# Where the later experts' token lists are read in a planned scan and mixture-of-experts kernel

## The chip, the core and the metric

The kernel runs on one core of a Trainium2 chip. The metric is the device time of one execution, in microseconds (us). Three runs of the kernel before stand beside one execution that the hardware profiler recorded.

## The reference

Three stages follow each other, all in float32.

```
x = gated linear scan(q, k, v, a_re, a_im)     # 4 batches, 8 heads, 768 steps, head size 48
x = (silu(g) * val) @ w_out,  g, val = rmsnorm(x) @ (w_gate, w_val)   # 3072 tokens, 384 -> 1536 -> 384
logits = x @ w_gate2;  e = argmax(logits);  p = softmax(logits)[e]    # 8 experts
out[token] = p * (relu(x @ w1[e]) @ w2[e])                            # 384 -> 1024 -> 384
```

Only the last stage is touched by the change. Each token goes to one of eight experts, so the kernel has to find out at run time which tokens an expert has, bring their rows together, run the two matrix products of that expert, and write the rows back to their places.

## The kernel before

The tokens are worked off in twelve units of 256 tokens. While a unit passes through the dense layer, its rows and logits go to `x2all` in DRAM, and a scatter on GpSimd's queue (L966) writes the number of each token into a list of its expert, in DRAM (`slots`, two tensors, one for each half of the unit). After the unit before the last, the experts are sorted by their counts so far (`sort`, L1033 to L1047); the place in that order is the number by which this text calls them: expert 0 is the largest one, 7 the smallest. Each has a fixed room for its tokens (`CAPS`); what goes beyond it is counted by `beyond` (L1049 to L1068) and worked off by a loop at the very end, which does not run when nothing went beyond.

An expert needs four things. Its **list**: `read_list` (L1124) issues two small loads from `slots` on SyncE's queue (SP, L1129), into one row of the two tiles `idx`, and VectorE joins the two by a minimum (L1132). Its **rows**: `gather` (L1136) issues one indirect load for each 110 to 128 tokens on GpSimd's queue (L1137, tile `ex`). Its **weights**: `load_weights` (L1091) loads seven pieces on SP's queue, three of `w1` (L1106, 512 KB each) and four of `w2` (L1108, 384 KB each), into three raw buffers (`rawb`) that are used in turn; ScalarE makes a rounded high part of each piece (L1113, `h1`, `h2`) and VectorE the rest (L1117, `l1`, `l2`), and only then is the raw buffer free for the load after the next two. And the **products**: TensorE transposes the rows (L1299, `ex`), ScalarE and VectorE split them into `exh` and `exl` (L1303, L1305), stage 1 makes eight column blocks (L1317, tile `m` in PSUM, three buffers), each split by ScalarE and VectorE into `ehh` and `ehl` (L1324, L1326), and stage 2 (L1335, tile `a` in PSUM, two buffers) makes the output, which ScalarE scales (L1341, `eo`) and GpSimd's queue scatters (L1343). Weights of experts with an odd number end in tiles that end in b, those of even ones in tiles that end in a.

Expert 0 is done in two halves: 246 tokens that were listed early (tiles `eh`, `el`), and 246 that are known late, whose rows are gathered into `rawa` and completed by rows of the last unit with matrix products by a selection matrix (`join_late`, L1182 and L1186). The list of expert 1 is completed in the same way (`join_next`), from the list of the units before the last. Experts 2 to 7 read their lists only after the last unit's scatters have landed.

No engine chooses its work at run time. Every instruction is recorded as a step with what it reads and writes, and `Plan.issue` (L185) then writes the instructions out engine by engine: again and again it takes, among the steps whose inputs are planned, one that can start first, ties going to the earlier due time. A step's cost and its `lag` (the time from the issue of a transfer to its landing) are the planner's estimates, and `after=` names further steps that have to be planned before it. All this sets only the order on each engine and queue; at run time each instruction waits for the data that it really touches, and all that stands behind it on its engine waits too. On the DMA queues a further wait is shown in some instructions: for an earlier transfer that uses the same completion semaphore.

Of the kernel before, what the change touches and what calls it, by code (L numbers as in the profile page):

```python
# [41 lines left out]
def act(n):  # L42
    return 0.1 + n / 1200


def dve(n):
    return 0.07 + n / 960


def pool2(n):  # L50
    return 0.15 + n / 460
# [82 lines left out]
class Plan:  # L134
# [5 lines left out]
    def add(self, engs, fn, r=(), w=(), due=0.0, table=None, lag=0.0, after=(), size=0, span=(0.0, math.inf), pull=0.0, lock=False):  # L140

        s = Step()
        s.size, s.span, s.pull, s.lock = size, span, pull, lock
        s.engs = [engs] if isinstance(engs, tuple) else engs
        s.fn, s.due, s.table, s.lag = fn, due, table, lag
        s.next, s.end, s.seq = [], None, len(self.steps)
        deps = {id(a): a for a in after}
        bufs = {}  # L150
        for writes, items in ((False, r), (True, w)):
            for x in items:
                b, part = x if isinstance(x, tuple) else (x, None)
                bufs[id(b)] = b
                for p, (wr, rd) in b.last.items():
                    if p == part or p is None or part is None:
                        for d in ([wr] if wr else []) + (rd if writes else []):
                            deps[id(d)] = d
        for writes, items in ((False, r), (True, w)):
            for x in items:  # L160
                b, part = x if isinstance(x, tuple) else (x, None)
                if writes:
                    if part is None:
                        b.last.clear()
                    b.last[part] = (s, [])
                else:
                    b.last.setdefault(part, (None, []))[1].append(s)
        deps.pop(id(s), None)
        s.bufs = list(bufs.values())
        for b in s.bufs:  # L170
            b.users += 1
        s.deps = list(deps.values())
        s.wait = len(s.deps)
        for d in s.deps:
            d.next.append(s)
        self.steps.append(s)
        return s
# [73 lines left out]
def kernel(ctx, tc, qT, kT, reT, imT, v, wg, wv, wo, rg, w2g, w1, w2, out):  # L251
    nc = tc.nc
    V, A, G, TE, SP = nc.vector, nc.scalar, nc.gpsimd, nc.tensor, nc.sync
    P = 128
# [19 lines left out]
    NJS = tuple(-(-c // P) for c in CAPS)  # L274
# [66 lines left out]
    add = plan.add  # L341

    def dma(fn, nbytes, r=(), w=(), due=0.0, after=(), issue=0.48, lag=TUNE["DL"]):
        return add((SP, issue), fn, r=r, w=w, due=due, lag=lag, size=nbytes, after=after)

    CNT, CARRY, X2ALL, SLOTS, IDENTR, GAIN, W2G, HOT, FIRST, PERM, MORE, SECOND = (Buf(t=1) for _ in range(12))
# [12 lines left out]
    def due_moe(u, f):  # L359
        return T0 + PER * u + FT * f  # L360
# [6 lines left out]
    def due_elem(u):  # L367
        return TUNE[f"EU{min(u, 5)}"] + (TUNE["E0"], T0 + TUNE["E1"], T0 + TUNE["E2"])[u] if u < 3 else T0 + PER * (u - 2) + TUNE["E3"]
# [291 lines left out]
    def attention(u, QK, vt):  # L660
        b, p = units[u]
        xh, xl = Buf(k_xh), Buf(k_xl)
        for c in range(NC):
            chunk(u, c, QK, vt, xh, xl, p == 0 and c == 0, p == NP - 1 and c == NC - 1)
        return xh, xl
# [342 lines left out]
    def due_e(x, i):  # L1008
        return due_moe(NU, 0) + sum(EP[:x]) + i - (TUNE["EL"] if x else 0.0)
# [66 lines left out]
        add((V, 0.1), lambda e: e.scalar_tensor_tensor(out=nk, in0=pc.t, scalar=SCALE, in1=rev,  # L1076
                                                       op0=ALU.mult, op1=ALU.add), r=[pc], w=[MORE], due=due)

    which, told = {}, {}

    def number(x, due):

        def load(e):
            i = x or E
            which[x] = nc.values_load(permi[0:1, i:i + 1], engines=[mybir.EngineType.SP], min_val=0, max_val=E - 1)

        return add((SP, 0.8), load, r=[PERM if x else FIRST], due=due)
# [3 lines left out]
    def load_weights(x, after):  # L1091
        W = [Buf(k) for k in k_w[x % 2]]
        if x not in told:
            told[x] = number(x, due_e(x, -32))
        after = after + [told[x]]
        for m, (src, n) in enumerate(((w1, KD), (w2, KF2 // 2))):
            for k in range(n):
                raw = Buf(k_rb if x else k_ra)
                due = due_e(x, 0) - EP[x - 1 if x else 0] + 4 * m + 0.4 * k - (40 if x == 1 else 0)

                def piece(t, m=m, k=k):
                    return t[:, k, :] if m == 0 else t[:, 2 * k:2 * k + 2, :].rearrange("p k d -> p (k d)")

                def load(e, raw=raw, m=m, k=k):
                    if m == 0:
                        e.dma_start(raw.t, w1r[bass.ds(which[x] * DM + k * P, P), :])  # L1106
                    else:
                        e.dma_start(raw.t[:, :2 * DM].rearrange("p (k d) -> p k d", k=2),  # L1108
                                    w2r[bass.ds(which[x] * F2 + 2 * k * P, 2 * P), :].rearrange("(k p) d -> p k d", p=P))

                cols = F2 if m == 0 else 2 * DM
                dma(load, P * cols * 4, w=[raw], due=due, after=after)
                add((A, act(cols)), lambda e, raw=raw, m=m, piece=piece, cols=cols: e.activation(  # L1113
                    piece(W[2 * m].t), raw.t[:, :cols], AF.Copy),
                    r=[raw], w=[(W[2 * m], k)], due=due, after=after)
                add([(V, dve(cols)), (G, pool2(cols))],
                    lambda e, raw=raw, m=m, piece=piece, cols=cols: e.tensor_tensor(  # L1117
                        out=piece(W[2 * m + 1].t), in0=raw.t[:, :cols], in1=piece(W[2 * m].t), op=ALU.subtract),
                    r=[raw, (W[2 * m], k)], w=[(W[2 * m + 1], k)], due=due, after=after, lock=True)
        return W  # L1120

    lists = [Buf(k) for k in k_idx]

    def read_list(x, row, lo, n, after):  # L1124

        due = due_e(x if x > 1 else 0, -30)
        at = [lambda b=b: b.t[:TPS[x], row, :n] for b in lists]
        for b, t, sl in zip(lists, at, slots):
            dma(lambda e, t=t, sl=sl: e.dma_start(t(), sl[bass.ds(which[x] * NT + lo, n * TPS[x]), :].rearrange(  # L1129
                "(p j) o -> p (j o)", j=n)), 2e3, r=[SLOTS], w=[(b, row)], due=due, after=after + [told[x]])  # L1130
        a, o = at
        add((V, 0.1), lambda e: e.tensor_tensor(out=a(), in0=a(), in1=o(), op=ALU.min),  # L1132
            r=[(lists[1], row)], w=[(lists[0], row)], due=due)
        return row

    def gather(X, j, idx, src, r, due, after, **kw):  # L1136
        add((G, 1.05), lambda e: e.indirect_dma_start(  # L1137
            out=X.t[:, j, :], out_offset=None, in_=src,
            in_offset=bass.IndirectOffsetOnAxis(ap=lists[0].t[:X.shape[0], idx, j:j + 1], axis=0), **kw),
            r=[(lists[0], idx)] + r, w=[(X, j)], due=due, lag=4.4, after=after)  # L1140

    def join_late(row, X):

# [116 lines left out]
    def expert(x, W, idx, n, rooms, due, after, X=None):  # L1260
# [14 lines left out]
        for j in () if there else range(n):  # L1275
            gather(X, j, idx, src, rows, due(-30), after)
# [71 lines left out]
    with tc.manual_schedule():  # L1348
# [31 lines left out]
        for sl in slots:  # L1380
# [11 lines left out]
            r=[GAIN], w=[GAIN], due=due_elem(0) + 1)  # L1392
        dma(lambda e: e.dma_start(w2gt[:, :, :E], w2g.rearrange("(k p) e -> p k e", p=P)), 1e3, w=[W2G],
            due=due_elem(0) + 1)
# [14 lines left out]
        for w, k in order[:int(TUNE["FF"])]:  # L1409
            add((TE, mmr(WB, int(TUNE["FN"]))), lambda e, w=w, k=k: keep_warm(e, w, k), r=[(w, 0), IDENTR], w=[fill],  # L1410
                due=1e6, span=(0.0, TUNE["W1"]))
        x = {0: attention(0, *q[0])}
# [4 lines left out]
        for u in range(NU):  # L1417
# [4 lines left out]
            if u + 1 == NU:  # L1422
                to_right = add((G, 0.0), open_right, after=[s for s in plan.steps if any(
                    b.slots and b.slots.where is right for b in s.bufs)], due=due_moe(u, 0))
                Wn = load_weights(0, [to_right])
            acc = dense(u, *x[u])
            if u + 1 == NU:
# [10 lines left out]
                idx1 = read_list(1, 1, 0, NJS[1], [to_right])  # L1438
# [11 lines left out]
        expert(0, Wn, late, NJ - NE, rooms1, lambda i: due_e(0, i), [to_left], Xl)  # L1450
        for x_ in range(1, E):
            W = load_weights(x_, [to_left])
            idx = idx1 if x_ == 1 else read_list(x_, x_, 0, NJS[x_], [to_right])
            expert(x_, W, idx, NJS[x_], rooms, lambda i, x_=x_: due_e(x_, i), [to_left])
        add((V, 2.0), beyond, r=[PERM, HOT], w=[MORE], due=due_e(2, 0))
        plan.issue()
        for cm in reversed(closers):
            cm.__exit__(None, None, None)
# [3 lines left out]
        with tc.For_i(0, nr, 1):  # L1462
            with tc.tile_pool(name="fb", bufs=1) as fb, tc.tile_pool(name="fp", bufs=2, space=PSUM) as fp:
# [30 lines left out]
                x = fb.tile([R, XW], F32, name="fx")  # L1494
# [30 lines left out]
                o = fb.tile([R, DM], F32, name="fo")  # L1525
# [49 lines left out]
```

## Time and profile before

| what | value |
|---|---|
| median of three runs | 958.65 us (954.86 to 959.91) |
| profiled execution | 958.0 us, of which the span from first to last instruction is 956.3 us |
| mean granted TensorE clock | 0.986 of 2.4 GHz |
| busy: PE, DVE, ACT, POOL | 95%, 66%, 55%, 17% of the span |
| DMA | 98.12 MB, mean 103 GB/s |

PE is TensorE's matmuls, DVE VectorE, ACT ScalarE, POOL GpSimd, SPq SyncE's DMA queue. Busy shares are means over the whole span. The experts' stage lies at its end: the last matmuls of the dense layer run until about 694 us, expert 0 is worked on from there, and the rest follow to the end. What an engine waits for there is read from the views of that stretch, in the section of rows below.

### The profile page before, as it was taken

The page shows a single profiled execution, that of the slowest core. Times are in us where ns is not written, and L with a number is a line of the kernel's source. Part 1 is how long each engine was busy: PE and PEld are TensorE (multiplying, and loading weights), DVE is VectorE, ACT ScalarE, POOL GpSimd, SP SyncE. Part 2 cuts the span into 40 slices and gives each one's busy share as a digit, 9 for nine tenths or more (in the row PEclk, how much of TensorE's full clock was granted, in tenths as well). Part 3 has the DMA queues.
Part 4 walks back from the last instruction along what each step waited for, and adds up shares of the span by engine and source line. Part 5 has one row for each costly group of instructions (what it writes and reads, how often), then busy time and mean ns, then how long its engine had stood idle before and what let it go on. Part 6 is the DMA issues. An engine that isn't in the chain of part 4 may idle for free.

```text
span 956.3 us, 17768 instructions
## 1 busy us (share of the span) xinstructions
PE 906.0 (95%) x6747; PEld 867.7 (91%) x6747; DVE 630.2 (66%) x1534; ACT 528.8 (55%) x1017; POOL 160.5 (17%) x211
## 2 busy tenths in 40 slices
PE   0979999999999999999999999999988999999996
PEld 0769999999999999999999999999877999999996
DVE  5889986878786969586868777446655543534520
ACT  8885775757575666565656575334424443544421
POOL 1223201010011010100101000101173142132121
PEclk9988999999999999999999999999999999999998
DMA  9932416151525060505050413003347554445200
GB/s 340 319 142 70 114 35 133 35 134 35 133 35 133 18 151 17 151 17 151 18 141 19 100 60 62 24 1 85 83 103 203 167 167 119 139 140 177 89 21 23
DMA packets 68363, 98.12 MB, mean 103 GB/s; under 512 B 16038, under 2 KB 49257, under 8 KB 68276
## 3 DMA queue, kind: packets, MB, share of 16 engines
q1 hardware_dynamic: 57316, 86.61, 32.7%
q0 software_dynamic: 10688, 9.95, 4.0%
q8 instruction: 54, 0.88, 0.4%
q10 hardware_dynamic: 272, 0.40, 0.1%
q14 instruction: 33, 0.27, 0.1%
HBM read 68.19 MB, written 10.15 MB: 82 GB/s over the span
## 4 chain that ended last, share of the span: by engine, by line
PE 62%; DVE 11%; issue 10%; ACT 7%; DMA 6%; SPq 2%; POOL 2%; POOLq 0%; DVEq 0%; ACTq 0%
PE m L868 26%; PE a L891 13%; PE a L1335 6%; PE t L698 4%; PE m L1317 3%; PE t L738 3%; DMA rawb<-in_w_dram 3%; DVE re L594 1%; PE t L742 1%; POOL out_dram L1343 1%; DVE ee L559 1%; PE t L716 1%; PE t L823 1%; DMA out_dram<-eo,idx 1%; DVE hl L885 1%
## 5 line engine op out<-in xcount | busy, mean ns | idle before, releaser
L868 PE MATMUL m<-xh,w 128*128 128x256 f32 x1728 | 278.6, 286 | 0.2 <-DVE s L880 0.2
L868 PEld LDWEIGHTS m<-xh,w 128*128 128x128 f32 x1728 | 236.3, 190 | 5.2 <-issue 3.6
L891 PE MATMUL a<-wo,hh 128*128 128x392 f32 (+1 forms) x576 | 152.6, 346 | 0.0
L868 PE MATMUL m<-xl,w 128*128 128x256 f32 x864 | 149.5, 282 | 0.0
L868 PEld LDWEIGHTS m<-xl,w 128*128 128x128 f32 x864 | 123.2, 190 | 0.0
L875 ACT ACTIVATE s<-m 128x256 f32<-128x256 f32 x144 | 54.3, 381 | 88.3 <-PE m L868 54.1
L891 PEld LDWEIGHTS a<-wo,hh 128*128 128x128 f32 x576 | 100.7, 189 | 0.6 <-issue 0.5
L891 PE MATMUL a<-wo,hl 128*128 128x392 f32 (+1 forms) x288 | 98.3, 341 | 2.3 <-DVE hl L885 2.3
L883 ACT ACTIVATE hh<-s 128x256 fp32r<-128x256 f32 x144 | 59.3, 416 | 64.1 <-PE a L891 43.7
L885 DVE TENSOR_TENSOR hl<-s,hh 128x256 fp32r<-128x256 f32 x144 | 63.8, 449 | 25.5 <-ACT hh L883 24.7
L877 DVE SCALAR_TENSOR_TENSOR s<-s,m 128x256 f32<-128x256 f32 x144 | 59.4, 415 | 24.4 <-ACT s L875 24.0
L1343 POOL DMA_INDIRECT out_dram<-eo,idx x28 | 37.1, 1327 | 162.6 <-ACT eo L1341 105.2
L1326 DVE SCALAR_TENSOR_TENSOR ehl<-m,ehh 128x384 fp32r<-128x384 f32 (+6 forms) x64 | 35.0, 555 | 42.1 <-ACT ehh L1324 42.1
L880 DVE SCALAR_TENSOR_TENSOR s<-s,m 128x256 f32<-128x256 f32 x144 | 59.4, 416 | 1.9
L1324 ACT ACTIVATE ehh<-m 128x384 fp32r<-128x384 f32 (+6 forms) x64 | 31.0, 491 | 48.9 <-PE m L1317 47.1
L1341 ACT ACTIVATE eo<-a,eg 114x384 f32<-114x384 f32 (+5 forms) x28 | 16.3, 581 | 73.4 <-PE a L1335 69.8
L891 PEld LDWEIGHTS a<-wo,hl 128*128 128x128 f32 x288 | 54.1, 188 | 2.9 <-DVE hl L885 2.9
L966 POOL DMA_INDIRECT slots<-tid,sl x24 | 25.1, 1046 | 150.7 <-DVE cnt L961 146.7
L738 PE MATMUL t<-AK,vt 128*64 128x224 f32 (+3 forms) x384 | 49.7, 345 | 0.0
L698 PE MATMUL t<-QK 96*128 96x128 f32 x384 | 48.1, 277 | 0.5 <-DMA QK<-ee 0.5
L698 PEld LDWEIGHTS t<-QK 96*128 96x128 f32 x384 | 45.5, 192 | 1.7 <-issue 0.9
L1335 PE MATMUL a<-h2b,ehh 128*118 128x384 f32 (+3 forms) x112 | 37.9, 339 | 0.0
(295 smaller groups left out, 1864.0 us busy)
## 6 DMA issues: line engine op xcount, KB each, us to landing
rawb<-in_w_dram SPq DMA_DIRECT2D x21, 512.0 KB, 7.5
rawb<-in_w_dram SPq DMA_DIRECT2D x28, 384.0 KB, 4.2
QK<-qk SPq DMA_DIRECT2D x24, 290.2 KB
QK<-ee SPq DMA_DIRECT2D x24, 290.2 KB, 6.4
re<-in_a_re_dram SPq DMA_DIRECT2D x12, 384.0 KB
im<-in_a_im_dram SPq DMA_DIRECT2D x12, 384.0 KB
qk<-in_q_dram SPq DMA_DIRECT2D x12, 384.0 KB, 5.1
qk<-in_k_dram SPq DMA_DIRECT2D x12, 384.0 KB, 5.8
```

What stands on the lines that cost most here:

```text
L698: TE.matmul(sc.t[:, i, :], lhsT=K(4 * g + i), rhs=Q(4 * g + i), start=True, stop=True)
L738: TE.matmul(yt.t[64 * n:64 * n + d, i, :n_], lhsT=vs[:, o:o + d], rhs=ak.t[:, 2 * i + n, :n_], start=True, stop=first)
L868: TE.matmul(ps.t[:, i, :], lhsT=W1[i, g].t[:, k, part, fs], rhs=x.t[:, k, :], start=(n == 0), stop=(n == 3 * KD - 1))
L875: add((A, act(U)), lambda e: e.activation(s.t, ps.t[:, 0, :], AF.Tanh, scale=0.5), r=[ps], w=[s], due=dh, table=AF.Tanh)
L877: add((V, dve(U)), lambda e: e.scalar_tensor_tensor(out=s.t, in0=s.t, scalar=1.0, in1=ps.t[:, 0, :], op0=ALU.add, op1=ALU.mult), r=[s, ps] ...
L880: add((V, dve(U)), lambda e: e.scalar_tensor_tensor(out=s.t, in0=s.t, scalar=0.5, in1=ps.t[:, 1, :], op0=ALU.mult, op1=ALU.mult), r=[s, ps ...
L883: add((A, act(U)), lambda e: e.activation(hh.t, s.t, AF.Copy), r=[s], w=[hh], due=dh)
L885: lambda e: e.tensor_tensor(out=hl.t, in0=s.t, in1=hh.t, op=ALU.subtract), r=[s, hh], w=[hl], due=dh, lock=True)
L891: TE.matmul(acc[t].t[:, :wide], lhsT=h.t[:, ts_], rhs=WO[g].t[:, k3, part, :wide], start=(f == 0 and n == 0), stop=(f == KF - 1 and n == 2))
L1326: add((V, dve(N)), lambda e, f=f, ps=ps: e.scalar_tensor_tensor(out=hl.t[:, f, :], in0=ps.t, scalar=0.0, in1=hh.t[:, f, :], op0=ALU.max, o ...
L1335: TE.matmul(po.t, lhsT=h.t[:, f, js], rhs=w.t[:, f, :], start=(f == 0 and i == 0), stop=(f == KF2 - 1 and i == 2))
L1343: add((G, 1.05), lambda e, o=o, j=j: e.indirect_dma_start(out=outs[(x + j) % len(outs)], out_offset=bass.IndirectOffsetOnAxis(ap=at(j), ax ...
```

## The change

Four things are changed, all of them in what the planner knows; no instruction is added or removed.

- The loads of weights are kept in a table, and the reading of expert x's list (x from 2) is planned only after a load of expert x-1's weights: for expert 2 after the last load of expert 1, for the others after the third load of the expert before.
- The lag of such a list's loads is put at 5.5 us instead of 2 (those of experts 0 and 1 keep 2).
- The lag of a gather is put at 6.5 us instead of 4.4.
- `beyond`, the count of what goes beyond the rooms, is planned after the third load of expert 3's weights.

```diff
-    which, told = {}, {}
+    which, told, loads = {}, {}, {}
...
-                dma(load, P * cols * 4, w=[raw], due=due, after=after)
+                loads.setdefault(x, []).append(dma(load, P * cols * 4, w=[raw], due=due, after=after))
...
-                "(p j) o -> p (j o)", j=n)), 2e3, r=[SLOTS], w=[(b, row)], due=due, after=after + [told[x]])
+                "(p j) o -> p (j o)", j=n)), 2e3, r=[SLOTS], w=[(b, row)], due=due, after=after + [told[x]], lag=5.5 if x > 1 else TUNE["DL"])
...
-            r=[(lists[0], idx)] + r, w=[(X, j)], due=due, lag=4.4, after=after)
+            r=[(lists[0], idx)] + r, w=[(X, j)], due=due, lag=6.5, after=after)
...
-            idx = idx1 if x_ == 1 else read_list(x_, x_, 0, NJS[x_], [to_right])
+            idx = idx1 if x_ == 1 else read_list(x_, x_, 0, NJS[x_], [to_right, loads[x_ - 1][-1 if x_ == 2 else 2]])
...
-        add((V, 2.0), beyond, r=[PERM, HOT], w=[MORE], due=due_e(2, 0))
+        add((V, 2.0), beyond, r=[PERM, HOT], w=[MORE], due=due_e(2, 0), after=[loads[3][2]])
```

What moves is seen in the order of the instructions. The first place is SP's queue where expert 1's weights begin. Before, the lists of experts 2 to 6 (the shapes 114x4, 110x4, 128x3, 128x3 and 122x3) stand ahead of the first piece of `w1`; the end of that run:

```order
L1129 DMA idx_8250<-slots_58 128x3
L1129 ISA
L1129 DMA idx_8272<-slots_59 128x3
L1129 ISA
L1129 DMA idx_8250<-slots_58 122x3
L1129 ISA
L1129 DMA idx_8272<-slots_59 122x3
L1106 ISA
L1106 DMA rawb_8901<-in_w_dram 128x1024
```

Now the same loads of weights follow at once on the five reads of the experts' numbers (L1085), and all seven of them, and two of expert 2, stand ahead of the first list (114x4, expert 2); a piece of it:

```order
L1085 TENSOR_LOAD permi
L1085 ISA x2
L1106 ISA
L1106 DMA rawb_8868<-in_w_dram 128x1024
L1106 ISA
L1106 DMA rawb_8880<-in_w_dram 128x1024
L1106 ISA
L1106 DMA rawb_8895<-in_w_dram 128x1024
L1108 ISA
L1108 DMA rawb_8966<-in_w_dram 128x2x384
```

The ten list loads have moved from ahead of these weights to between the later experts' weights. The second place is DVE in the late half of expert 0. Before, the join of expert 4's list (L1132) stands ahead of the weight of the gate (L1285 to L1287) and of the three `exl`:

```order
L1326 SCALAR_TENSOR_TENSOR el_8724<-m_8853,eh_8709 128x246
L1132 TENSOR_TENSOR idx_8250<-idx_8250,idx_8272 128x3
L1285 TENSOR_REDUCE eg_8891<-eg_8891 123x2
L1286 TENSOR_SCALAR eg_8891<-eg_8891 123x2
L1287 RECIPROCAL eg_8891<-eg_8891 123x2
L1305 TENSOR_TENSOR exl_8924<-t_8894,exh_8907 128x246
```

Now nothing stands between:

```order
L1326 SCALAR_TENSOR_TENSOR el_8724<-m_8835,eh_8709 128x246
L1285 TENSOR_REDUCE eg_8870<-eg_8870 123x2
L1286 TENSOR_SCALAR eg_8870<-eg_8870 123x2
L1287 RECIPROCAL eg_8870<-eg_8870 123x2
L1305 TENSOR_TENSOR exl_8902<-t_8873,exh_8886 128x246
```

The joins of the lists have gone further back on DVE, and `beyond`, which stood ahead of the two L1186, with them. The third place is DVE in expert 1, where the joins for experts 2 (114x4) and 3 (110x4) now stand, and behind the second one the first use of expert 2's gathered rows (L1280):

```order
L1117 TENSOR_TENSOR l1a_9140<-rawb_9092,h1a_9128 128x1024
L1132 TENSOR_TENSOR idx_8250<-idx_8250,idx_8272 114x4
L1117 TENSOR_TENSOR l1a_9140<-rawb_9123,h1a_9128 128x1024
L1326 SCALAR_TENSOR_TENSOR ehl_9196<-m_9111,ehh_9192 128x472
L1326 SCALAR_TENSOR_TENSOR ehl_9196<-m_9130,ehh_9192 128x472
L1326 SCALAR_TENSOR_TENSOR ehl_9196<-m_9182,ehh_9192 128x472
L1326 SCALAR_TENSOR_TENSOR ehl_9196<-m_9206,ehh_9192 128x472
L1132 TENSOR_TENSOR idx_8250<-idx_8250,idx_8272 110x4
L1280 TENSOR_REDUCE eg_9260<-ex_9162 114x4
```

Expert 2's gathers, which GpSimd's queue had ahead of all scatters of expert 0, now stand behind the two of them.

## Rows read from the trace of the kernel before

**Rows 1.** PE's longest waits, 660 to 957 us: total, times, longest in us.

```profile
PE m L1317 <- DVE exl L1305: 3.9, 1, 3.9
PE a L1335 <- ACT eo L1341: 3.2, 1, 3.2
```

**Rows 2.** PE's timeline, 707 to 748 us: start, us, instruction, [idle before <-releaser].

```profile
707.88 0.79 PE L1299 MATMUL t<-ident,rawa 123*128 123x123 f32 x6
...
714.97 1.21 PE L1317 MATMUL m<-exl,h1a 128*128 128x246 f32 x3 [3.86 <-DVE exl L1305]
...
718.49 0.51 PE L1317 MATMUL m<-exh,h1a 128*128 128x246 f32 x3
...
720.57 0.34 PE L1335 MATMUL a<-h2a,eh 128*123 128x384 f32 x1
...
722.23 0.61 PE L1317 MATMUL m<-exh,h1a 128*128 128x246 f32 x3 [0.96 <-DVE ehl L1326]
...
728.22 0.34 PE L1335 MATMUL a<-h2a,ehh 128*123 128x384 f32 x1
...
732.45 0.81 PE L1317 MATMUL m<-exh,h1b 128*128 128x472 f32 x3
...
739.71 0.68 PE L1335 MATMUL a<-h2a,ehh 128*123 128x384 f32 x1 [3.23 <-ACT eo L1341]
...
746.72 0.81 PE L1317 MATMUL m<-exh,h1b 128*128 128x472 f32 x3
```

**Rows 3.** DVE's timeline, 700 to 716 us.

```profile
701.24 0.20 DVE L1054 TENSOR_TENSOR grid<-rank,rev 1x64 f32<-1x64 f32 x1
...
704.09 1.04 DVE L1186 TENSOR_TENSOR rawa<-t,rawa 123x392 f32<-123x392 f32 x2
...
713.96 0.16 DVE L1132 TENSOR_TENSOR idx<-idx,idx 128x3 int32<-128x3 int32 x1 [5.59 <-DMA idx<-slots]
...
714.53 1.03 DVE L1305 TENSOR_TENSOR exl<-t,exh 128x246 fp32r<-128x246 f32 x3
```

**Rows 4.** Stages: us, then busy of PE, PEld, DVE, ACT, POOL, clock, DMA, GB/s.

```profile
715.00:718.50 3.50, 3.50 (x16) 3.43 (x17) 1.21 (x5) 0.38 (x1) 0.00 (x0) 0.51 1.00 270
...
739.70:745.60 5.90, 5.89 (x18) 5.89 (x19) 3.45 (x4) 3.02 (x3) 1.52 (x1) 0.50 0.63 173
```

**Rows 5.** ACT's timeline, 690 to 745 us.

```profile
738.34 0.84 ACT L1113 ACTIVATE h2b<-rawb 128x768 fp32r<-128x768 f32 x1 [6.59 <-DMA rawb<-in_w_dram]
```

**Rows 6.** SP's queue, 685 to 735 us (merged: from the first to the last issue).

```profile
690.80 19.57 SPq L1129 DMA_DIRECT2D idx<-slots  x12
710.63 4.87 SPq L1106 DMA_DIRECT2D rawb<-in_w_dram  x3
...
721.88 6.64 SPq L1108 DMA_DIRECT2D rawb<-in_w_dram  x4
```

**Rows 7.** Chain that ended last, 640 to 957 us: start, us, what.

```profile
698.25 4.60 DMA slots<-tid,sl
...
754.40 7.72 PE m L1317 x36
```

**Rows 8.** Line 1085 on SP: ns min/median/max, first and last start in us.

```profile
L1085 SPq SEQ_ASSERT  x8: 18/18/33, 648.4 to 694.7; - x8
```

**Rows 9.** Tile rawb: ns min/median/max of its operations, first and last start.

```profile
L1113 ACT ACTIVATE h1b<-rawb x12: 1047/1054/1068, 719.5 to 888.4; 128x1024 fp32r<-128x1024 f32 x12
L1117 DVE TENSOR_TENSOR l1b<-rawb,h1b x12: 1217/1225/1226, 720.6 to 889.9; 128x1024 fp32r<-128x1024 f32 x12
...
DMA to landing us min/median/max: 3.2/5.0/8.0
```

**Rows 10.** Tile ex: from a gather's issue to its landing.

```profile
DMA to landing us min/median/max: 3.8/6.2/9.5
```

**Rows 11.** Stage of the last gathers for expert 0: columns as in rows 4.

```profile
694.00:702.00 8.00, 8.00 (x68) 7.37 (x67) 5.94 (x31) 2.25 (x6) 5.73 (x6) 1.00 0.29 88
```

**Rows 12.** POOL's timeline, 640 to 957 us.

```profile
696.46 1.49 POOL L1137 DMA_INDIRECT rawa<-x2all,idx  x1 [0.30 <-issue]
```

## The prediction

> **What bounds the kernel now.** I read PE's waits over the experts' stage first, then PE's timeline around each of them, then the engine that each names, and last the queue behind that engine. PE is busy for 95% of the span, so the end moves only by what PE loses. Over the last 300 us two of its waits are longer than 3 us [rows 1], and both lie in expert 0 and at the start of expert 1.
>
> The first is in the late half of expert 0. PE stands 3.86 us until 714.97 for `exl` [rows 2]. `exl` is late because DVE stood still for 5.59 us, until 713.96, at the join of expert 4's list, which its queue has ahead of the gate's weight and of `exl` (714.53) [rows 3]. After that gap the clock is granted at 0.51, the lower of its two levels (1.2 GHz), from 715 to 718.5 [rows 4]: 18 matmuls take 718.49 - 714.97 = 3.52 us, where the next 18 of the same shape take 720.57 - 718.49 = 2.08 [rows 2]. That is 1.44 us more, so this place costs 3.86 + 1.44 = 5.30 us.
>
> A small one follows: 0.96 us at 722.23, for `ehl`, with DVE in the middle of expert 1's weights.
>
> The second large one is at 739.71: 3.23 us for `eo` [rows 2]. ACT had been idle for 6.59 us, until 738.34, for the last piece of expert 1's weights, which stands ahead of `eo` on its queue [rows 5]. The clock is then at 0.50 from 739.7 to 745.6 [rows 4], and 24 matmuls of stage 2 take 746.72 - 739.71 = 7.01 us, where 24 of the same shape took 732.45 - 728.22 = 4.23 [rows 2]: 2.78 us more, 6.01 in all.
>
> Why are those weights late? On SP, twelve list loads take the queue from 690.80 to 710.37, and only then come expert 1's first three pieces, at 710.63 [rows 6]. Inside that stretch the queue stands until the last unit's scatter has landed, 698.25 + 4.60 = 702.85 [rows 7], since the lists of experts 2 to 7 need it and the weights, which don't, are behind them. The fourth and later pieces begin at 721.88 only.
>
> **The change part by part.** The span's own time is 956.3 us in an execution of 958.0; the median is 958.65, so I take differences from the trace and set them against the median.
>
> *The list joins leave the front of DVE's queue.* With nothing between, `exl` follows the last `el`. The lists themselves cost SP about as much as before, but later. Removed: the 3.86 us and, if the clock stays up, the 1.44.
>
> *Expert 1's weights go ahead of the lists.* SP is free when the last of the experts' numbers is read, 694.7 [rows 8]; the wait for TensorE that the first piece has is for a matmul of the dense layer long past. So the three pieces of `w1` start at about 694.8, 16 us earlier, and land by 699.8 at the median of 5.0 us, by 702.8 at the worst of 8.0 [rows 9]. ACT and DVE come to them only after the first column of the late half, which in the new run ends near 711.7, so what now sets the pace is their own work: 1.05 us for a high part, 1.23 for a rest [rows 9], with a column's split between. Three rounds of that end near 717.5 on DVE, and each frees a raw buffer for a piece of `w2`: loads at about 714.5, 716.1, 717.6 and, after the first `l2`, 720.3, where they were issued from 721.88 to 728.5 [rows 6]. The fourth lands between 723.5 (3.2 us) and 728.3 (8.0). PE will want `eo` not before 739.71 - 3.23 - 5.30 - 0.96 = 730.2. So the 3.23 us go, and with the gap the 2.78.
>
> *What is late next, first place.* ACT's new order puts three high parts of `w2` between the three `exh` of expert 1. PE wants the first column of expert 1 at 732.45 - 5.30 - 0.96 = 726.2. The third of these pieces lands between 720.8 and 725.6, and behind it stand 0.84 us of its own [rows 5], a column's split, the last `exh` and the last `exl`, an estimate of 2.6 us together. So this costs between 0 and 725.6 + 2.6 - 726.2 = 2.0 us; in between lies nothing else on the queues but one scatter, so I take 0.8.
>
> *Second place: expert 2's list and rows.* The list is read after expert 1's four `w2` and two pieces of expert 2's `w1`, at about 724; DVE joins it behind the second `l1a`, near 730, and GpSimd's queue issues four gathers from then to about 735. They land at 741 at the median of 6.2 us, at 744.5 at the worst of 9.5 [rows 10]. DVE now has the first use of these rows (L1280) ahead of three weight parts and of the split for PE's fourth column. That column began before at 754.40 + 3/4 * 7.72 = 760.2 [rows 7], so in the new run between 747 and 748; with an estimated 3.7 us of DVE's work between, the rows are free until 743.3, so this costs 0 to 1.2 us, and I take 0. The lists of experts 3 to 7 stand behind weights on which DVE waits anyway; I find no row there where a list would be the last to land.
>
> *`beyond`.* Its twelve small operations take 704.09 - 701.24 = 2.85 us ahead of L1186 [rows 3]. Moved to where expert 2's matmuls run for over 10 us without DVE, they cost nothing there; taken away here they give nothing, since the transposes that use L1186's result come at 707.88 [rows 2]. If that cover were gone, 2.85 us is the price.
>
> *Longer lags.* A planner's figure takes no time; what it moved is in the places above, and the early half's gate, moved by a few places in the dense layer, has no wait of PE beside it.
>
> The 0.96 us: PE's third buffer of `m` comes back in time by my count, with 0.1 us to spare. I take all of it, with 0 as the other end.
>
> Sum: 5.30 + 0.96 + 6.01 - 0.8 = 11.5 us. 958.65 - 11.5 = 947.1. Bounds of this case: 12.3 if nothing new waits, 5.30 + 6.01 - 2.0 - 1.2 - 1.0 = 7.1 if the new places and the contention below cost their worst and the 0.96 stays.
>
> **Contention, weighed.** The weights' 1.5 MB now fall between 694.8 and about 702, where the DMA engines were busy for 0.29 of the time [rows 11], so there is room; but the last gathers of expert 0 are in flight there, the later one issued at 696.46 [rows 12], with 6.2 us to land [rows 10]. At the 270 GB/s of a full stretch [rows 4] 1.5 MB take 5.7 us: that is the most by which a gather could be put back, from 702.7 to 708.4. L1186 behind it needs half of its 1.04 [rows 3], and PE wants it at 707.88, so PE would wait 1.0 us. The bounds are 0 and 1.0; I take 0, because the engines are idle for 0.71 of that stretch. The Trainium skill (DMA: Bandwidth & Descriptors, Queues, rings and completion order) says that each engine takes turns between the queues that have work, a packet at a time. By that rule a gather is put back by a packet or two and not by the whole 1.5 MB, and the sum would stay at 11.5; if a gather had to stand behind all of it, the sum would be 10.5. No row here shows both kinds in flight at full load with their own times.
>
> **The rivals.**
>
> Rival A: one of the two large losses comes back as a new wait. For it: ACT's new order has a wait for a transfer in it, and `eo` and `exh` stand behind. Against: the transfers start 7 to 8 us earlier against a need that is 6 us earlier. If PE stands over 3 us once and the clock falls as it did at 739.71, 6.0 us are lost again: 11.5 - 6.0 = 5.5 us gained, 953.1; with half of that, 950.
>
> Rival B: the change does nothing. The weights start earlier, but DVE's and ACT's work on them takes the same turns as before, and expert 1's last piece stays late by what the column splits cost. Then only the first place goes and the later place takes its gain back: 958.65 - 1.0 to - 4.5, 954 to 958.
>
> Rival C, slower: expert 2's rows. The list stands behind two pieces of expert 2's weights, and these behind parts that DVE makes behind a load. Each us by which the four gathers land after 743.3 is a us of PE, and past 3.3 us of it the clock adds 2.8. The gain of 11.5 is used up when they land at 743.3 + 11.5 - 2.8 = 752, and 0.5% beyond that, 4.8 us, at 757: 966 us for a landing at 760. For it: DVE can't pass over L1280. Against: that is 25 us after the issue, and the worst here is 9.5 [rows 10].
>
> **How the numbers follow.** A measurement of this kernel can't tell a change within 0.5%, 4.8 us, from none. My forecast (7.1 to 12.3 us gained, 946.4 to 951.5) has 0.62; with the spread of the runs, some 2.5 us to either side, it is seen between 943.9 and 954. Rival A has 0.20, three quarters of it past 0.5%; B 0.11; C 0.07, of which 0.04 is slower by over 0.5%. More than I count (the small waits of 0.9 us elsewhere) lies in the forecast's lower end. Range 943.5 to 954: it leaves out B and C and the end of A. Faster by over 0.5%: 0.62 + 0.20 * 0.75 + a little of B = 0.80; slower 0.05; the rest, 0.15, the same.
>
> **What would show it.** Right: no wait of DVE for `idx` ahead of `exl`; loads of `rawb` on SP from about 695; no wait of PE for `eo` in expert 1, and the granted clock at full from 710 to 750; expert 1's first column near 726 and the last matmul some 11 us earlier. Wrong: ACT idle for a transfer ahead of `exh` or `eo` near 720 to 730 (A); DVE idle at L1280 near 740 with PE waiting for `ehl` after it (C); `el` or L1186 late for gathers near 705 (contention).

## The result, and the profile after

The changed kernel takes 946.84 us (median of six executions, 944.79 to 948.68), the kernel before 958.1 beside it (six, 954.86 to 961.25). The ratio is 0.988, with a 95% interval of 0.9855 to 0.9908: 11.3 us faster, 947.1 was predicted. The profiled execution took 948.68 us, with a span of 946.9.

That execution is the slowest of its six, and it shows where from: 2.66 us are lost before the change has done anything. PE's first transposes of the late half's rows start at 710.54 us here, at 707.88 before [rows 2]. To compare the two, 2.66 is taken from the times after this point ("in the time of before"). From these transposes to PE's last matmul it is 240.6 us before and 938.76 - 710.54 = 228.2 after.

PE's waits behind 690 us, by what was waited for (total, number, longest). There were two over 3 us [rows 1]; now:

```profile
PE a L891 <- DVE hl L885: 2.0, 1, 2.0
PE m L1317 <- DVE ehl L1326: 1.5, 1, 1.5
```

Neither `exl` nor `eo` is left. The granted clock (the column behind POOL's) is full through the whole stretch of both losses, but not just ahead of it:

```profile
688.00:690.00 2.00, 0.76 (x6) 0.43 (x4) 1.70 (x10) 0.92 (x4) 0.00 (x0) 1.00 0.43 132
692.00:694.00 2.00, 2.00 (x8) 2.00 (x7) 1.70 (x6) 1.15 (x2) 0.00 (x0) 0.50 0.06 2
710.00:730.00 20.00, 20.00 (x146) 19.74 (x145) 14.03 (x32) 12.26 (x26) 6.10 (x4) 1.00 0.57 163
730.00:750.00 20.00, 19.90 (x102) 18.10 (x101) 11.35 (x20) 9.61 (x15) 12.74 (x11) 1.00 0.75 203
```

The 0.50 at 692 stands behind a wait of 1.99 us that the kernel before has too, with 1.70 and no drop. The wait is 0.29 us longer, the matmuls behind it take 1.6 us more, and 0.8 us are drift from earlier: together the 2.66.

SP's queue (start, time to the last issue, count), to be held against [rows 6]:

```profile
691.90 0.76 SPq L1129 DMA_DIRECT2D idx<-slots  x2
696.04 1.48 SPq L1106 DMA_DIRECT2D rawb<-in_w_dram  x3
717.13 6.94 SPq L1108 DMA_DIRECT2D rawb<-in_w_dram  x4
725.45 1.77 SPq L1106 DMA_DIRECT2D rawb<-in_w_dram  x2
727.42 0.81 SPq L1129 DMA_DIRECT2D idx<-slots  x2
```

Expert 1's weights start at 696.04 instead of 710.63, and expert 2's list comes behind nine pieces: expert 1's seven and two of expert 2. On ACT the rows that answer to [rows 5]:

```profile
714.80 1.05 ACT L1113 ACTIVATE h1b<-rawb 128x1024 fp32r<-128x1024 f32 x1
728.48 0.84 ACT L1113 ACTIVATE h2b<-rawb 128x768 fp32r<-128x768 f32 x1 [2.32 <-DMA rawb<-in_w_dram]
729.23 0.56 ACT L1341 ACTIVATE eo<-a,eg 123x384 f32<-123x384 f32 x1
```

ACT still idles for the last piece, 2.32 us, but `eo` is done by 729.79, and PE starts its next group of stage 2 at 731.98 only (below). On DVE, [rows 3] have become:

```profile
706.09 1.04 DVE L1186 TENSOR_TENSOR rawa<-t,rawa 123x392 f32<-123x392 f32 x2 [2.10 <-DMA rawa<-x2all,idx]
711.44 1.03 DVE L1305 TENSOR_TENSOR exl<-t,exh 128x246 fp32r<-128x246 f32 x3
744.96 0.19 DVE L1280 TENSOR_REDUCE eg<-ex 114x4 f32<-114x32 f32 x1 [2.10 <-DMA ex<-x2all,idx]
748.23 0.64 DVE L1326 SCALAR_TENSOR_TENSOR ehl<-m,ehh 128x472 fp32r<-128x472 f32 x1
```

`exl` has no list ahead of it. Two waits for gathers are new, at L1186 and at L1280, and PE feels neither. PE's first rows of expert 1, stage 1, and of the next group of stage 2:

```profile
728.11 0.81 PE L1317 MATMUL m<-exh,h1b 128*128 128x472 f32 x3
...
731.98 0.34 PE L1335 MATMUL a<-h2a,ehh 128*123 128x384 f32 x1
```

Expert 1's first column starts at 728.11, which is 725.45 in the time of before; 726.2 was predicted without a cost of the first new place, 727.0 with it.

### The profile page after: what moved, and what is told of

Same layout as the page of the kernel before. It is cut to its first block, busy times and chain, and to the rows that moved or that the text cites. A ratio compares the mean times of both kernels' runs of the same rounds, so it can differ in the third digit from the quotient of the medians.

```text
span 946.9 us, 17768 instructions
## 1 busy us (share of the span) xinstructions
PE 901.3 (95%) x6747; PEld 863.8 (91%) x6747; DVE 630.0 (67%) x1534; ACT 528.9 (56%) x1017; POOL 158.8 (17%) x211
## 4 chain that ended last, share of the span: by engine, by line
PE 65%; DVE 11%; issue 8%; ACT 7%; DMA 6%; POOL 1%; SPq 1%; POOLq 0%; DVEq 0%; ACTq 0%
PE m L868 26%; PE a L891 14%; PE a L1335 6%; PE m L1317 5%; PE t L698 4%; PE t L738 3%; DMA rawb<-in_w_dram 2%; DVE re L594 1%; PE t L742 1%; DMA out_dram<-eo,idx 1%; DVE ee L559 1%; PE t L716 1%; DMA QK<-ee 1%; POOL out_dram L1343 1%; DVE hl L885 1%
```

## The experiments

My theory: both losses come from where the lists stand, on SP ahead of the weights and on DVE ahead of `exl`; beyond and the lags cost and give nothing. The first rival: the planner's lags, or beyond's new place, carry a part. The second: new waits (late rows, contention) have taken something back. All times are medians; the kernel before was timed beside each, at 956.42 us beside the first four runs, 956.05 beside the next four and 957.1 beside the last four.

**The lists' place alone (e1).** The kernel before with this line (and the table of loads that it reads):

```
-  read_list(x_, x_, 0, NJS[x_], [to_right])
+  read_list(x_, x_, 0, NJS[x_], [to_right, loads[x_ - 1][-1 if x_ == 2 else 2]])
```

> The kernel before with one part of the change alone: the later lists are read behind weights of the expert ahead of them; the planner's lags and beyond stay as before. My theory: both large losses (5.30 + 0.96 us for exl and ehl, 6.01 us for eo) come from the lists' place on SP's queue and from their joins on DVE's, so this part alone gives all of the gain: 958.1 - 11.5 = 946.6 (944.5 to 948.5), PE without a wait for exl and for eo, and beyond (2.85 us on DVE ahead of L1186) hidden behind the gathers that L1186 waits for anyway. Rival 1, beyond has to move too: L1186 ends 2.85 us later and PE waits 1 to 2.9 us for the transposes behind it, 948 to 950.5. Rival 2, the lags carry the first part (without them a join comes back ahead of exl): PE waits some 3.9 us for exl and the gain is 6 us, 952.

Measured: 945.5 us, ratio 0.9894 (0.9866 to 0.9922), the gain of the whole change within the intervals. PE has no wait for `exl` or `eo`, and one of 0.61 us for expert 1's rows. The lists' place is enough.

**The lags alone (e2).** The kernel before with

```
-  after=after + [told[x]])
+  after=after + [told[x]], lag=5.5 if x > 1 else TUNE["DL"])
-  due=due, lag=4.4, after=after)
+  due=due, lag=6.5, after=after)
```

> The kernel before with the planner's two lags alone (5.5 us for the later lists, 6.5 us for a gather); the lists stay ahead of expert 1's weights on SP, and beyond stays. On DVE the late half's gate and exl then stand ahead of the joins. My theory: the wait for exl goes, but the weights still start at 710.6, so PE only comes to eo some 6 us earlier and waits that much longer there (6 to 9 us instead of 3.2, with the clock at its lower level behind it): the gain is given back but for what DVE frees earlier, 0 to 4 us, so 954 to 958. Rival, the two losses are independent: 6.3 us are gained and the wait for eo stays 3.2 us, 951.8.

Measured: 952.69 us, ratio 0.9972 (0.995 to 0.9994), between the two expectations, and neither had the place right. PE's waits over 1 us behind 700 us in this run:

```profile
723.01 0.60 PE L1317 MATMUL m<-exh,h1a 128*128 128x246 f32 x3 [3.04 <-DVE ehl L1326]
743.02 0.91 PE L1317 MATMUL m<-exh,h1b 128*128 128x472 f32 x3 [1.10 <-DVE ehl L1326]
```

`exl` is in time, since DVE has it ahead of the joins. The loss comes back 8 us later: ACT stands for expert 1's first weights, and the high part that PE waits for stands behind them:

```profile
720.32 1.06 ACT L1113 ACTIVATE h1b<-rawb 128x1024 fp32r<-128x1024 f32 x1 [3.78 <-DMA rawb<-in_w_dram]
721.28 0.36 ACT L1324 ACTIVATE ehh<-m 128x246 fp32r<-128x246 f32 x1
```

The clock is granted at 0.50 from 724 to 726 behind that gap. The wait for `eo` is gone, because the planner now has `eo` ahead of the last `h2b`. So DVE's order carries the first loss, and SP's order, which is here as before, the second; but a late weight shows wherever ACT's queue has it next: I had named `eo`, it was `ehl`. (No run moved the lists on SP and left the joins on DVE, so the second half rests on these traces.) From the late half's transposes to the last matmul it is 233.5 us here.

**Without the lags (e3).** The changed kernel with the old lags.

```
-  lag=5.5 if x > 1 else TUNE["DL"]      -  lag=6.5
+  (the default)                         +  lag=4.4
```

> The changed kernel with the planner's old lags (lists 2.8 and gathers 4.4 us as the code before had them): lists behind weights, beyond moved. My theory: the lags carry none of the two losses, so the time is that of the changed kernel within 1.5 us: 945.3 to 948.3, without a wait of PE for exl or eo. Against the run with the lists' place alone it differs only by where beyond stands, so the two tell beyond's price: 0 by my count, up to 2.9 us if beyond was on the way. Rival, the lags matter: DVE's joins or gates then stand too early and PE waits 1 us or more somewhere from 700 to 760, 949 or more.

Measured: 946.54 us, 0.9907 (0.9877 to 0.9937), as expected (the lists' old lag is 2 us, not 2.8). e1 and e3 differ only by `beyond`; 945.5 against 946.54 is within both intervals, so its price is 0 as far as this can tell.

**The changed kernel again (e4).**

> The changed kernel once more, on the same chip as the three others and with a profile of its own. The median should be 946.8 (945 to 948.5). The profile shown of it had PE's clock at 0.50 from 692 to 694 behind a wait of 1.99 us for hl, which the kernel before did not have behind a wait of 1.70. If that stretch is a matter of the execution and not of the change, it comes and goes between profiles of one kernel (the order of the work there is nearly the same), and an execution without it has about 1.5 us less. If the change causes it, it is in this profile too.

Measured: 946.6 us, 0.99 (0.9871 to 0.9928). Its profile has 1.39 us at 690 and no drop of the clock there: the dip at 692 comes and goes between executions of one kernel. Whether the change makes it more frequent is not shown. But it has one behind the wait for `ehl` near 781, 2.20 us long here and 1.52 in the first profile:

```profile
780.00:782.00 2.00, 1.09 (x3) 0.98 (x4) 1.94 (x4) 0.64 (x2) 0.00 (x0) 0.78 0.38 100
782.00:784.00 2.00, 2.00 (x7) 1.71 (x6) 0.00 (x0) 0.00 (x0) 0.00 (x0) 0.50 0.51 172
```

Its cause is on ACT, where `h2b` of expert 3's last piece stands ahead of the high parts of PE's columns:

```profile
773.15 0.55 ACT L1324 ACTIVATE ehh<-m 128x456 fp32r<-128x456 f32 x1 [1.30 <-PE m L1317]
778.48 0.84 ACT L1113 ACTIVATE h2b<-rawb 128x768 fp32r<-128x768 f32 x1 [4.78 <-DMA rawb<-in_w_dram]
779.23 1.41 ACT L1324 ACTIVATE ehh<-m 128x456 fp32r<-128x456 f32 x3
```

**Weights behind the last write (e5).**

```
-  dma(load, P * cols * 4, w=[raw], ...)
+  dma(load, P * cols * 4, r=[(X2ALL, NU - 1)] if x == 1 and m == 0 else [], w=[raw], ...)
```

> The changed kernel, with one wait more: expert 1's three w1 loads on SP wait until the last unit's rows have landed in x2all; the order of every engine stays. In the changed kernel that write took 697.06 to 706.23 us beside 1.5 MB of weights (694.39 to 696.91 in the kernel before), and the last gathers of expert 0 landed at 706.4 instead of 702.7. My theory: these are put back by the weights, so with the weights behind, the write lands within 2 to 4 us of its issue, the gathers near 702 to 704, expert 1's rows some 4 us earlier than 720.9; the weights land near 705 to 708, before ACT wants them at 714.8. Nothing of that was on PE's path, so the time stays at 946.6 (945.3 to 948). Rival 1, the contention did cost something: 0.5 to 1.5 us faster. Rival 2, the weights are now late: PE waits 1 to 3 us for ehl behind them, 948 to 950.

Measured: 945.31 us, 0.9896 (0.9873 to 0.9919). This tested nothing: the edit tells only the planner of a dependence, every engine's order came out the same, the loads do not wait, and SP issues them at 693.54 as ever. It is the changed kernel a third time. Holding the weights back was not tried otherwise; e11 below shows the gathers with the weights out of their way.

**Rows late, first try (e6).**

```
+  [e.memset(X.t, 0.0) for _ in range(3 * (idx == 2 and j == 0))]    (ahead of the gather)
```

> The changed kernel with three memsets of expert 2's row buffer on GpSimd ahead of its four gathers (some 1.5 us each, 4.5 to 5 in all; the gathers overwrite it), the order of the other engines unchanged. This tests the prediction's second new late place and rival C's price. In the changed kernel's profile the last of these gathers landed at 744.84, DVE went on at 744.96, and PE wanted the result of the split behind it, ehl (done at 748.9), at 749.8: 1.0 us to spare. My theory (DVE can't pass over L1280): a landing near 749.6 makes PE wait 3.5 to 4 us for ehl, and the clock falls behind that for 1.4 to 2.8 us more: 951.5 to 953.5. Rival, there is more slack than that, because only the gate needs these rows so early: no wait of PE over 1 us, 947.

Measured: 943.78 us, 0.9873 (0.985 to 0.9895), and no wait of PE in expert 1:

```profile
728.74 4.39 POOL L1137 MEMSET ex<- 114x1568 f32 x3
733.43 1.50 POOL L1137 DMA_INDIRECT ex<-x2all,idx  x1 [0.31 <-POOL ex L1137]
```

The memsets filled time in which GpSimd had been idle for the join. Counted from the late half's transposes (706.88 here), the gathers come 2.5 us later than in the changed kernel, and DVE's L1280, at 742.52, only 1.2: just what there was to spare. It doesn't decide between the theories, so it was done again as e9.

**The splits ahead of the sort (e7).** The wait at 690 is for three splits `hl` that stand behind twelve small operations of `sort` on DVE; here `sort` follows them.

```
+  add((V, 2.0), sort, ..., after=[hls[u, f] for f in range(KF - 2)])    (behind the last dense unit)
```

> The changed kernel with DVE's twelve small operations that sort the experts by size put behind the three splits hl of the dense layer that stood behind them. In five profiles PE waited 1.4 to 2.0 us for the first of these at 690 us, and in one the clock was at 0.50 for 3 us after it. My theory: the wait goes to under 0.5 us and the time falls by 1.2 to 1.9 us, to 944.7 to 945.4; the number of expert 1 comes 1.1 us later on SP, and its weights with it, which costs nothing. Rival: what moved on DVE (the early half's splits now ahead of the last unit's routing) makes lists, gathers and L1186 later, and PE waits for exl or el by as much as it gained: 946 to 948.

Measured: 945.63 us, 0.9898 (0.9869 to 0.9928). The wait at 690 is gone, but the time is the changed kernel's (945.31 beside it, in e5): the gain of 1.2 to 1.9 us did not show. The profile has the wait near 779 at 2.21 us, and the clock falls behind it as in e4, to a mean of 0.83 from 780 to 790. (Of the six profiles before this run, the first one and e1's had the clock at 0.50 behind the wait at 690.)

**Both (e8).** As e7, and

```
+  lag=7.0 if x == 3 and m and k == 3 else TUNE["DL"]     (the landing of one w2 piece, for the planner)
```

> As the run with the splits ahead of the sort, and the planner's figure for the landing of expert 3's last w2 piece raised from 2.0 to 7.0 us; ACT then has two high parts ehh of PE's columns ahead of that piece's h2b. In profiles of the changed kernel ACT stood 4.8 us for this piece (issued about 770, landed 778.4 to 780.1), the ehh behind it, and PE waited 1.5 to 2.2 us for ehl at 781 to 783, in one profile with the clock at its lower level behind it. My theory: that wait goes too, another 1.5 to 2.5 us: 942.5 to 944. Rival: h2b is then late for stage 2 of expert 3 and the wait comes back there, 944.7 to 946.

Measured: 942.13 us (four executions, 940.61 to 942.61), 0.9852 (0.9827 to 0.9877), the fastest here. PE's only wait over 0.3 us behind 684:

```profile
PE t L1299 <- DMA ex<-x2all,idx: 0.4, 1, 0.4
```

and ACT has the high parts ahead of the piece it waits for:

```profile
775.00 0.55 ACT L1324 ACTIVATE ehh<-m 128x456 fp32r<-128x456 f32 x1 [1.30 <-PE m L1317]
776.43 0.85 ACT L1113 ACTIVATE h2b<-rawb 128x768 fp32r<-128x768 f32 x1 [0.88 <-DMA rawb<-in_w_dram]
```

**Rows late, second try (e9).** As e6, with five memsets between the first gather and the other three.

> The test of late rows again, since the first one did not make them late: its memsets ran while GpSimd was idle for the join, and the gathers began as before. Now five memsets of 1.1 us each (from the 4.39 us of three of 1568 elements) stand behind the first of expert 2's four gathers, so the last three come 5.5 us later whatever the join does. In the changed kernel's profile the last landed at 744.84, DVE went on at 744.96, and 1.0 us was to spare until PE wanted ehl. My theory (DVE can't pass over L1280): PE waits 4 to 5 us for ehl in expert 1, the clock falls behind that for 1.4 to 2.8 us more, 951.5 to 954.5. Rival, there is more slack: no wait of PE over 1 us there, 946 to 947.5.

Measured: 951.85 us, 0.9949 (0.9923 to 0.9975): 5 us over the changed kernel. DVE and then PE:

```profile
748.84 0.19 DVE L1280 TENSOR_REDUCE eg<-ex 114x4 f32<-114x32 f32 x1 [8.16 <-DMA ex<-x2all,idx]
```

```profile
752.48 1.55 PE L1317 MATMUL m<-exh,h1b 128*128 128x472 f32 x3 [3.73 <-DVE ehl L1326]
```

The clock is at 0.51 from 752 to 754. DVE goes on 3.9 us later than in the changed kernel, 4.8 when both are counted from the late half's transposes (709.66 here); PE waits 3.73. That is the 1.0 us of slack, then a us for a us, then the clock: rival C's price, which the change itself came within 1 us of.

**All three (e10).** e8 with the edit of e5.

> A version meant to beat both: the changed kernel with the three splits hl ahead of the sort, with 7.0 us for the landing of expert 3's last w2 piece, and with expert 1's first weights behind the last unit's write to x2all. Without the third edit its profile had one PE wait over 0.3 us behind 684 us, 0.42 for expert 1's rows, whose gathers start after that write has landed. My theory: that goes, and the time falls by 0.3 to 0.6 us against 942.1: 941 to 942.5. Rival: with the number of expert 1 1.1 us later and the weights behind the write, the weights are late for ACT and PE waits 1 us or more for ehl: 943 to 945.

Measured: 943.77 us, 0.9853 (0.9817 to 0.989), not the forecast. By what e5 showed this is e8's program again, so the third edit was not tested. Its profile has 0.68 us for expert 1's rows, and a wait that e8's has not:

```profile
736.34 0.91 PE L1317 MATMUL m<-exh,h1b 128*128 128x472 f32 x3 [1.14 <-DVE ehl L1326]
```

By the ratios the two are 0.3 to 0.5% faster than the changed kernel, with intervals that still overlap.

**Expert 2's list first (e11).**

```
-  [to_right, loads[x_ - 1][-1 if x_ == 2 else 2]]
+  [to_right] + ([loads[x_ - 1][2]] if x_ > 2 else [])
```

> The changed kernel, with expert 2's list read ahead of expert 1's weights as before, and the lists of experts 3 to 7 behind weights. SP then stands for the last unit's scatter (landed at 706.65 in the changed kernel, 702.85 in the one before), reads two of the twelve loads, and starts the weights some 9 us later than in the changed kernel, at 703.5 to 705.5. My theory: they land by 710 to 713.5, ACT wants the first at 714.8, so nothing waits and the time is 946.6 (945 to 948): what cost time was the ten other list loads, not the scatter. Rival 1, the weights' start counts: PE waits 1 to 3 us for ehl, 948 to 950. Rival 2, the late landing of expert 2's rows had cost something: 0.5 us or more faster.

Measured: 948.27 us, 0.9924 (0.9888 to 0.996). My theory had it wrong; the time and the waits are rival 1's, though the interval overlaps the changed kernel's, and it is the waits below that decide. SP stands for the scatter, and the weights start at 703.43, 10.5 us later than in the changed kernel when both are counted from the late half's transposes (707.41 here):

```profile
690.30 12.93 SPq L1129 DMA_DIRECT2D idx<-slots  x4
703.43 2.57 SPq L1106 DMA_DIRECT2D rawb<-in_w_dram  x3
```

ACT then waits for each of the three, the last at

```profile
717.55 1.06 ACT L1113 ACTIVATE h1b<-rawb 128x1024 fp32r<-128x1024 f32 x1 [1.38 <-DMA rawb<-in_w_dram]
```

and PE for `ehl`, 0.37, 0.34 and 1.40 us. I had let them land within 8 us. They took some 9.2 (by ACT's start), 10.8 and 12.9, with expert 1's gathers and, from 710, expert 2's in flight beside them; expert 1's gathers took 11.3 to 14.7 us here and 7.8 to 9.2 in the changed kernel. The run moves both the weights' start and expert 2's gathers, so it doesn't tell their shares.

**The kernel before again (e12).**

> The kernel before once more, with a profile of its own. Its shown profile was of an execution of 958.0 us and lost 12.3 us in two places of expert 0 and 1, by which I sized the gain; the medians of the runs so far differ by 9.6 to 11.3 us. If those losses are the same in every execution, this profile shows PE waiting 3.6 to 4.1 us for exl, some 1 us for ehl and 3.0 to 3.5 us for eo, with the clock at its lower level behind the two large ones, and the rest of the difference lies ahead of 690 us. Rival: they vary with the landings, and the sum in this execution is 9 to 10 us.

Measured: 956.8 us, 1.0001 (0.9976 to 1.0025). Its three waits in the stretch:

```profile
716.20 1.22 PE L1317 MATMUL m<-exl,h1a 128*128 128x246 f32 x3 [3.73 <-DVE exl L1305]
723.12 0.61 PE L1317 MATMUL m<-exh,h1a 128*128 128x246 f32 x3 [0.40 <-DVE ehl L1326]
739.68 0.44 PE L1335 MATMUL a<-h2a,ehh 128*123 128x384 f32 x1 [2.29 <-ACT eo L1341]
```

The first is stable (3.86 and 3.73), the other two are smaller than in [rows 1 and 2]: from the late half's transposes to the last matmul it is 237.9 us here, 240.6 in the profile that the prediction read. The rival was right: the sum varies with the landings.

## Why the prediction was right

**The first loss, 5.30.** As said: `exl` follows the last `el`, the clock is full. e2 shows that DVE's order alone takes it away; e12 that its size is steady. The term itself was miscounted. Between 714.97 and 718.49 in [rows 2] stand 15 matmuls, three to a row, and not 18:

```profile
714.97 1.21 PE L1317 MATMUL m<-exl,h1a 128*128 128x246 f32 x3 [3.86 <-DVE exl L1305]
715.99 0.85 PE L1317 MATMUL m<-exh,l1a 128*128 128x246 f32 x3
716.63 0.84 PE L1317 MATMUL m<-exh,h1a 128*128 128x246 f32 x3
717.27 0.84 PE L1317 MATMUL m<-exl,h1a 128*128 128x246 f32 x3
717.91 0.75 PE L1317 MATMUL m<-exh,l1a 128*128 128x246 f32 x3
```

At the rate of the 18 behind them (2.08 us) 15 take 1.73, so the clock cost 1.79 us instead of 1.44, and the place 5.65.

**The small one, 0.96.** Gone; it was 0.40 in e12, so its usual size is smaller.

**The second loss, 6.01.** The place was right, the size was that of one execution. In e12 the wait is 2.29 instead of 3.23, and the stretch from expert 1's first column to expert 2's first transposes 2.1 us shorter than in the first profile: some 3.9 in all. The sum of 12.3 (12.6 with the right count) was that of the worse of two profiles; the three places of e12 cost some 10 us.

**First new place, 0.8.** Not paid. ACT's `h2b` stood between the `exh`; the first of them waited 0.68 us for its transfer, the next two did not, and PE did not wait at all.

**Second new place, 0.** Paid 0 by PE, as taken, with DVE's wait of 2.10 and 1.0 us to spare. The landing came at 744.84, or 742.2 in the time of before, 1.2 later than said, and the edge was where it was put: 744.96 + 1.0 - 2.66 = 743.3. e9 shows that the price behind that edge was real.

**`beyond` and the lags, 0.** e1 and e3 agree. In e1 `beyond` stands ahead of L1186, where its operations take 1.92 us, and PE loses nothing there; 2.85 was one execution's.

**Contention, 0 taken and 1.0 as the bound.** PE paid nothing, but the transfers were not left alone. The last gathers of expert 0 (count, median us from issue to landing), first in the changed kernel, then in e11, where the weights start after they have landed:

```profile
rawa<-x2all,idx POOLq DMA_INDIRECT x2, 9.5
```

```profile
rawa<-x2all,idx POOLq DMA_INDIRECT x2, 5.9
```

Three other profiles with the weights out of the way have 5.9 to 6.2, five with them beside 8.7 to 9.7. So in the changed kernel 1.5 MB put these gathers back by 3.3 to 3.6 us, which is more than half of the 5.7 that a stand behind all of it would cost. The Trainium skill (DMA: Bandwidth & Descriptors, Queues, rings and completion order) has the engines take turns packet by packet; the delay of a packet or two was my reading of it, and isn't what these traces show. The delay stayed off PE's path: L1186 ran at 706.09, and PE comes to its result at 710.54. Only expert 1's rows, which come behind the same transfers, cost PE something in three profiles: 0.61 us in e1, 0.42 in e8 and 0.68 in e10.

**Rival A.** A large loss that comes back is what e2 shows for the lags alone; in the changed kernel's profile PE has no wait over 0.3 us between 700 and 780.

**Not in the sum.** The wait for `ehl` near 782, 0.91 before (0.79 in e12) and 1.5 to 2.2 in four profiles of the changed kernel and of its order, with the clock down behind the longest (e1, where ACT waits 2.16 us for that piece and not 4.09 as in the changed kernel's first profile, has none). It gives back 0.6 to some 3 us. This, and the size of the second loss, lower the gain; the 0.8 that wasn't paid raises it. The kernels' stretches from the late half's transposes on are 240.6 and 237.9 before, 228.2, 230.1 and 227.9 after (the first profile, e4, e5): 10.5 us between the means, where 11.5 were said. The medians say 11.3 for the first pair, 9.8 for e4 and 10.7 for e5. So the mechanism was right, and that 946.84 lies within 0.3 us of 947.1 is in part luck: the terms that were too large and too small nearly cancel, and the gain itself differs by 1.5 us from pair to pair.

## What to carry to other kernels

A load that waits for nothing should not stand on a queue behind loads that wait; moving it costs nothing if what it overtakes has slack, and that slack is to be measured (here 1.0 us, found by making the rows late). A wait that is taken away at one place can come back at another operation of an in-order queue as long as the late transfer itself isn't moved: with the lags alone the wait for the weights on ACT went from `eo` to `ehh`. Losses of waits are to be sized from more than one profile: one of the two here was a third smaller in the next.

## What the runs showed that was not expected

Gaps of PE and the clock behind them: at 690 us gaps of 1.37 to 1.70 us (eight profiles) left the granted clock at full speed, and in all three profiles with 1.93, 1.99 and 2.05 it fell to the lower level, 0.50 in the first profile, for some 3 us. Near 780, gaps of 1.51 to 2.01 left it, 2.20 and 2.21 did not. Rival C had the clock fall only behind waits of over 3.3 us; these gaps are shorter. A wait that varies by 0.5 us between executions can thus vary by about 2 us in what it costs (the 1.99 us of the first profile cost 1.6 more in the matmuls behind it).

Whether a small write is issued just ahead of a large load or inside it seems to count too. Expert 1's gathers need the last unit's rows. In three profiles (the first one, e1 and e9) the write of these rows went out 1.0 us behind the first weight piece (697.06 against 696.04 in the first one), and the first of these gathers started 10.1 to 10.2 us after the write's issue, at 707.19 in the first one. In seven others the write went out 0.5 to 0.6 us ahead of that piece, and the gather started 7.2 to 9.0 us after it (in e4 695.08 and 702.30). In all four profiles in which the weights come later, it is 7.2. The three are also those with the clock's drop at 690, behind which the write comes later on ACT. No run moved the write by itself, so this is an observation and not a shown cause.
